# Six row tiles in the last FFN chunk, block 12 in Strassen form, and work moved across the chunk seams

## The chip, the cores and the metric

One core of one Trainium2 chip. The metric is the device time of one execution in microseconds, median over runs.

Names: PE is TensorE, DVE is VectorE, ACT is ScalarE, POOL is GpSimd. The FFN runs over 16 row tiles of 128 rows. I call its chunks 0 (tiles 0, 1), A (2 to 5), B (6 to 9), C (10 to 13) and D (14, 15); the change replaces C and D by one chunk E (10 to 15).

## The reference, cut to what matters

```python
x = A_x                                             # (1, 2048, 640), bf16
h = layernorm(x) * (1 + ca) + sa
x = x + ga * irfft2(rfft2(h) * (w_r + 1j * w_i))    # not touched (with LN2 and chunk 0 it fills the first 104 us)
h = layernorm(x) * (1 + cb) + sb                    # LN2
x = x + gb * ((silu(h @ w_gate) * (h @ w_up)) @ w_down)   # 640 -> 1728 -> 640
```

1728 hidden columns are 13 blocks of 128 (0 to 12) and 64 left over.

## The kernel before

Gate and up are computed together by a seven-product Strassen scheme: one 2x2 side is (gate, up), the other is the two halves of a chunk's rows; the sums of weights (`GS`, `UG`) are made once, the sums of row halves (`h_sums`) per chunk. Blocks 0 to 11 go through it in pairs; block 12 and the 64 columns (`gu13`) are done plainly. Down is Strassen again, over pairs of row tiles.

```python
chunks = [(0, 2), (2, 4), (6, 4), (10, 4), (14, 2)]     # first tile, number of tiles

def gate_up_pairs(ci, ATc, extra):
    n = chunks[ci][1]
    F, M = 8 // n, 64 * n          # blocks in a group, columns of a product
    nG = 12 // F
    # step(0) X = w*b11, copied out by ACT      step(1) Y = GS0*t1 + ..
    # step(2) X += GS1*t2, copied out           step(3) Z = w*b21 + ..,  DVE c11 = Z + c0
    # step(4) X += GS2*t3, copied out as c3,    DVE c22 = Y + c3
    # step(5) Y += GS3*b22 + ..,                DVE c12 = Y + c2
    # step(6) X += w*t4 + .., two silu (ACT),   DVE first half of rows = c11 * g21
    # step(7) DVE second half of rows = c12 * g22
    for p in range(nG):
        step(0, p); step(5, p - 2); step(4, p - 1); step(7, p - 2)
        if p and extra: extra.pop(0)()
        if p == 0: fin13 = gu13(ci, ATc)
        step(1, p); step(2, p); step(6, p - 1)
        if n == 4: queue(p - 1)              # sums for the down product, run in turns
        if p < nG - 1: step(3, p); run(8 // n)
        if p == 1: fin13()
    half = gu_plain(ci, ATc, 12, tmp[nG % 2])      # block 12, plain
    step(5, nG - 2); step(4, nG - 1); step(7, nG - 2); step(3, nG - 1)
    # ... (n == 2 has an order of its own)
    run(2); half(0); step(6, nG - 1); half(1, lambda: run(len(later)))
    # ...

for ci, (t0, n) in enumerate(chunks):
    # ... gate and up ...
    if ci == 1:                                    # LN2 variances of tiles 10 to 15
        ln2_var(10, 6); ln2_pow(10, 6); ln2_nb(10, 6)      # DVE, POOL, DVE
    if ci + 1 < len(chunks): ln2_tr(ci + 1)        # transposed load of the next chunk
    for j in range(n // 2):
        # a pair of tiles; in the last one DVE also runs ln2_mod and h_sums of the next chunk
        down_pair(ATc, t0 + 2 * j, j, nxt)
```

The PSUM banks are taken in turn from a ring of eight (`next_banks`).

## Time and profile before

252.05 us, median of three runs (251.85 to 252.06); the traced run took 250.93 us. The trace from A's first product on, one row a chunk; the columns are the stretch and its length, then busy time and (number) of PE, of PE's weight loads, of DVE, ACT and POOL, then the granted clock and the DMA's share and rate:

```profile
104.37:144.56 40.19, 40.19 (x331) 32.13 (x330) 35.82 (x76) 26.56 (x48) 8.12 (x7) 1.00 0.13 29
144.56:184.76 40.20, 40.20 (x331) 32.06 (x330) 35.27 (x77) 24.29 (x45) 5.42 (x6) 1.00 0.15 35
184.76:224.95 40.19, 40.19 (x332) 32.15 (x331) 33.29 (x75) 21.62 (x41) 5.43 (x6) 1.00 0.10 26
224.95:245.73 20.78, 20.68 (x284) 18.34 (x281) 16.50 (x41) 10.51 (x20) 0.00 (x0) 1.00 0.07 21
```

A, B and C take the same time although their DVE and ACT load differs by 2.5 and 5 us: PE sets it. D's two tiles cost 10.4 us each, the others' 10.05.

Before A's first product lie 104.37 us, after the last row 3.4 us for the last output and its transfer. The last row runs to the output add that follows D's last product; up to that product's end, at 245.70, D takes 20.75 us.

### The profile page before, as it was taken

How to read it: one execution, taken by the hardware profiler on the slowest of the kernel's cores; microseconds unless marked ns; L12 is line 12 of the kernel's file. 1: busy time of each engine (PE TensorE's matmuls, PEld its weight loads, DVE VectorE, ACT ScalarE, POOL GpSimd, SP SyncE). 2: the span in 40 equal slices, each digit the busy share in tenths (PEclk: the TensorE clock that was granted, in tenths of full speed). 3: DMA queues.
4: the chain of work that ended last, by engine and by line, in shares of the span. 5: the costliest groups of instructions: out<-in, count | busy, mean ns of one | idle time of the engine just before them, and what ended most of it. 6: DMA issues, size and time to landing. Idle time of an engine off the chain costs nothing.

```text
span 249.1 us, 6473 instructions
## 1 busy us (share of the span) xinstructions
PE 243.5 (98%) x2512; PEld 200.4 (80%) x2512; DVE 209.7 (84%) x524; ACT 162.7 (65%) x300; POOL 74.3 (30%) x122
## 2 busy tenths in 40 slices
PE   8999999999999999999999999999999999999994
PEld 3778877999889888688877778886768887779973
DVE  4798888998898997879997997879995888895895
ACT  3778666997788798488862487674356766235740
POOL 8487755894025422000003900001330000440000
PEclk9999999999999999999999999999999999999999
DMA  7999999999999999300005020003311000211001
GB/s 221 396 357 334 309 365 191 175 397 381 286 352 288 275 264 186 81 9 0 3 0 108 13 68 29 3 3 58 73 42 39 3 0 3 54 53 57 3 0 53
DMA packets 45760, 34.43 MB, mean 138 GB/s; under 512 B 21731, under 2 KB 42658, under 8 KB 45346
## 3 DMA queue, kind: packets, MB, share of 16 engines
q1 hardware_dynamic: 43936, 30.00, 42.8%
q0 software_dynamic: 1504, 3.95, 6.7%
q8 instruction: 19, 0.31, 0.5%
q10 hardware_dynamic: 290, 0.08, 0.1%
q14 instruction: 11, 0.09, 0.1%
HBM read 26.72 MB, written 4.72 MB: 126 GB/s over the span
## 4 chain that ended last, share of the span: by engine, by line
PE 80%; SPq 9%; DMA 6%; ACT 1%; DVE 1%; issue 1%; DVEq 0%; ACTq 0%
PE psum L1016 33%; PE psum L899 19%; PE psum L986 9%; DMA rW<-wflip_r 4%; PE psum L879 3%; PE psum L597 3%; PE psum L664 3%; PE psum L567 2%; SPq L273 2%; SPq L277 2%; PE psum L1149 2%; DMA rM<-in_w_mod_dram 2%; SPq L275 2%; PE psum L1152 2%; PE psum L974 2%; PE psum L618 2%
## 5 line engine op out<-in xcount | busy, mean ns | idle before, releaser
L1016 PEld LDWEIGHTS <-rW 128*128 128x128 bf16 (+1 forms) x528 | 46.9, 98 | 5.6 <-issue 0.2
L1016 PE MATMUL psum<-rW 128*128 128x256 bf16 (+1 forms) x240 | 27.1, 259 | 0.0
L913 POOL TENSOR_TENSOR rM<-rM,rL 128x320 f32<-128x320 f32 x6 | 5.9, 975 | 68.2 <-ACT rL L912 68.2
L899 PEld LDWEIGHTS <-rE 128*128 128x128 f16 (+1 forms) x196 | 19.1, 97 | 7.7
L1016 PE MATMUL psum<-rY,rW 128*128 128x256 bf16 (+1 forms) x96 | 24.0, 259 | 0.0
L986 PE MATMUL psum<-rW 128*128 128x256 bf16 (+1 forms) x170 | 23.1, 291 | 0.0
L899 PE MATMUL psum<-rE 128*128 128x320 f16 (+1 forms) x147 | 22.3, 299 | 0.0
L590 DVE TENSOR_TENSOR rM<-psum,rW 128x384 bf16<-128x384 f32 (+2 forms) x42 | 20.1, 541 | 2.0 <-PE psum L567 1.4
L986 PEld LDWEIGHTS <-rW 128*128 128x128 bf16 x170 | 16.6, 98 | 3.8
L1016 PEld LDWEIGHTS <-rE 128*128 128x128 f16 x192 | 17.4, 98 | 2.4
L899 PEld LDWEIGHTS <-rX 128*128 128x128 bf16 (+1 forms) x151 | 14.6, 97 | 5.4
L760 POOL TENSOR_TENSOR rstd<-rstd,mhalf 128x4 f32<-128x4 f32 (+2 forms) x4 | 4.5, 1120 | 48.2 <-DVE rstd L756 48.2
L1052 DVE TENSOR_TENSOR rH<-psum,rW 128x512 bf16<-128x512 f32 x21 | 14.5, 689 | 4.9 <-PE psum L1016 3.1
L1048 ACT COPY rH<-psum 128x512 f32<-128x512 f32 x21 | 12.3, 585 | 9.0 <-PE psum L1016 7.3
L1042 ACT COPY rW<-psum 128x512 f32<-128x512 f32 x21 | 12.3, 585 | 6.8 <-PE psum L1016 6.7
L1055 ACT COPY rX<-psum 128x512 f32<-128x512 f32 x21 | 12.3, 586 | 6.7 <-PE psum L1016 6.7
L1070 DVE TENSOR_TENSOR rX<-rH,rL 128x512 bf16<-128x512 bf16 x21 | 8.9, 423 | 9.1 <-ACT rL L1068 9.0
L382 DVE SCALAR_TENSOR_TENSOR rE<-rE,mv,psum 128x648 bf16<-128x648 f32 (+1 forms) x17 | 14.2, 844 | 2.1 <-PE psum L318 1.5
L1056 DVE TENSOR_TENSOR rX<-psum,rX 128x512 f32<-128x512 f32 x21 | 14.4, 685 | 1.7 <-ACT rX L1055 1.6
L899 PE MATMUL psum<-rA,rX 128*128 128x320 bf16 (+1 forms) x98 | 15.6, 299 | 0.0
L1016 PE MATMUL psum<-rH,rW 128*128 128x256 f16 (+1 forms) x96 | 15.1, 259 | 0.1
L1016 PE MATMUL psum<-rE,rY 128*128 128x256 f16 (+1 forms) x96 | 15.1, 259 | 0.0
(198 smaller groups left out, 674.3 us busy)
## 6 DMA issues: line engine op xcount, KB each, us to landing
out_dram<-rA SPq DMA_DIRECT2D x31, 80.0 KB, 1.6
rM<-in_w_mod_dram SPq DMA_DIRECT2D x3, 800.0 KB, 9.9
rX<-in_A_x_dram SPq DMA_DIRECT2D x3, 640.0 KB, 7.3
rA<-in_B_w_down_dram SPq DMA_DIRECT2D x2, 960.0 KB, 14.4
rM<-in_w_mod_dram SPq DMA_DIRECT2D x1, 1600.0 KB, 7.1
rY<-in_B_w_gate_dram POOLq DMA_DIRECT2D x2, 768.0 KB, 7.7
rW<-in_B_w_gate_dram SPq DMA_DIRECT2D x2, 640.0 KB, 7.2
rW<-in_B_w_up_dram SPq DMA_DIRECT2D x2, 640.0 KB, 6.5
```

What stands on the lines that cost most here:

```text
L382: nc.vector.scalar_tensor_tensor(Zv[:, h], Cv[:, h], mv[:, t, 0:1], zps[:, h], ALU.mult, ALU.subtract)
L590: nc.vector.tensor_tensor(PP[:, :, hl], xv[:, :, hl], in1, ALU.mult)
L597: nc.tensor.matmul(yps[:, i, :], lhsT=_rev(PP, 64 * n * ps + i, [[n, 128]]), rhs=identb[:], start=(ps == 1 and i == 0), stop=(ps == 0 and ...
L899: nc.tensor.matmul(o, lhsT=lhsT, rhs=rhs, start=start, stop=stop, skip_group_check=True)
L986: nc.tensor.matmul(gu[u], lhsT=Wgu[:, u, c5, ff * 128:(ff + 1) * 128], rhs=h2T[:, :, c5, :], start=(c5 == 0), stop=(c5 == NC5 - 1))
L1016: nc.tensor.matmul(o[:, f], lhsT=w, rhs=b, start=(start and f == 0 and i == 0), stop=(stop and f == F - 1 and i == len(ops) - 1), skip_gro ...
L1042: nc.scalar.copy(c0, X)
L1048: nc.scalar.copy(c2, X)
L1052: nc.vector.tensor_tensor(c11, Z, c0, ALU.add)
L1055: nc.scalar.copy(c3, X)
L1056: nc.vector.tensor_tensor(c22, Y, c3, ALU.add)
L1070: nc.vector.tensor_tensor(ato, v4(c11), v4(g21), ALU.mult)
```

## The change

The intent: give PE fewer and wider matmuls. C and D become one chunk of six tiles; block 12 joins the Strassen scheme as a group of its own at the head of each chunk; the first down products are begun between the last group's, where block 12's plain products had stood; the last variances move from A's down part into A's third group. Room for the larger chunk is found in the rows of x1 that are already output.

```diff
-    chunks = [(0, 2), (2, 4), (6, 4), (10, 4), (14, 2)]
+    chunks = [(0, 2), (2, 4), (6, 4), (10, 6)]
-    def gate_up_pairs(ci, ATc, extra):
+    def gate_up_pairs(ci, ATc, extra, dn):
-        F, M = 8 // n, 64 * n
-        nG = 12 // F
+        M = 64 * n
+        groups = [[12]] + ([[f, f + 6] for f in range(6)] if n == 4
+                           else [[f + 6 * s] for f in range(6) for s in range(2)])
+        L = len(groups) - 1
 ...
+            if p == 2 and ci == 1:
+                ln2_var(10, 6)
+                ln2_pow(10, 6)
 ...
-        half = gu_plain(ci, ATc, 12, tmp[nG % 2])
-        step(5, nG - 2)
-        step(4, nG - 1)
-        step(7, nG - 2)
-        step(3, nG - 1)
+        step(5, L - 1)
+        step(4, L)
+        step(7, L - 1)
+        step(3, L)
 ...
+            run(2)
+            dn = dn()
+            dn.head(0)          # down: X, blocks 0 to 3
+            step(6, L)
+            dn.head(1)          # X, blocks 4 and 6
+            run(len(later))
+            queue(L)
+            later.extend([lambda: step(8, L), lambda: step(7, L)])
+            step(5, L, True)
+            dn.head(2)          # Y, blocks 0 to 3
+            run(len(later))
 ...
+    def at_of(ci):
+        A = rM.cut(4096, [NFC * N]) if chunks[ci][1] == 6 else AT[:, 0:NFC * N]   # x1's rows
 ...
-        if ci == 1:
-            ln2_var(10, 6)
-            ln2_pow(10, 6)
-            ln2_nb(10, 6)
```

The rest is addresses, the 1664 columns of the tables in place of 1536, tiles 14 and 15 normalized and transposed during B, and a guard that drops four useless sums at the start of each chunk of four.

More of the change, by code (lines that the diff above doesn't have):

```diff
@@ L743, in adaln_block_kernel @@
     nb2 = const.tile([P, NT], F32, name="nb2")
-    h2T_first, h2T_next = rW.cut(45056, [2, NC5, 128]), rW.cut(33280 + 512, [4, NC5, 128])
-    xn2c = rL.cut(4096, [4, D])
-    chunks = [(0, 2), (2, 4), (6, 4), (10, 4), (14, 2)]
+    h2T_first, h2T_next = rW.cut(38912, [2, NC5, 128]), rW.cut(33280 + 512, [6, NC5, 128])
+    xn2c, xn2x = rL.cut(4096, [4, D]), rM.cut(5120, [2, D])
+    chunks = [(0, 2), (2, 4), (6, 4), (10, 6)]
     def ln2_sq(t):
@@ L770, in ln2_xn_act, with ln2_tr @@
         t = chunks[ci][0] + i
-        nc.scalar.activation(xn2c[:, i, :], x1[:, t, :], ACT.Identity, scale=rstd2[:, t:t + 1], bias=nb2[:, t:t + 1])
+        nc.scalar.activation(xn2c[:, i, :] if i < 4 else xn2x[:, i - 4, :], x1[:, t, :], ACT.Identity, scale=rstd2[:, t:t + 1], bias=nb2[:, t:t + 1])
     def h2T_of(ci):
         return (h2T_next if ci else h2T_first)[:, 0:chunks[ci][1]]
-    def ln2_tr(ci):
-        n = chunks[ci][1]
+    def ln2_tr(ci, lo=0):
+        n = min(chunks[ci][1] - lo, 4)
         nc.sync.dma_start_transpose(
-            h2T_of(ci).rearrange("p tl c q -> p (tl c) q"),
-            xn2c[:, 0:n].rearrange("p tl (c q) -> p (tl c) q", c=NC5))
+            h2T_of(ci)[:, lo:lo + n].rearrange("p tl c q -> p (tl c) q"),
+            (xn2x if lo else xn2c)[:, 0:n].rearrange("p tl (c q) -> p (tl c) q", c=NC5))
     def ln2_mod(ci, cs=range(NC5)):
@@ L793, in ln2_mod @@
                                      scale=one_p_cb[:, c5:c5 + 1], bias=modcols[:, 2, c5:c5 + 1])
-    GS = [r.cut(off, [2, 1536], F16) for r, off in ((rY, 0), (rE, 25600), (rW, 38912), (rE, 31744))]
-    UG = rH.cut(1280, [1536], F16)
+    GC = 13 * 128
+    GS = [r.cut(off, [2, GC], F16) for r, off in ((rY, 0), (rE, 25088), (rW, 42496), (rE, 31744))]
+    UG = rH.cut(1280, [GC], F16)
     def gu_w(u, k):
-        return Wgu[:, u, 2 * k:2 * k + 2, 0:1536]
+        return Wgu[:, u, 2 * k:2 * k + 2, 0:GC]
     def gu_table(i, q):
-        fs = slice(512 * q, 512 * q + 512)
+        fs = slice(512 * q, 512 * q + 512 if q < 2 else GC)
         s1, s2, s4 = (GS[k][:, :, fs] for k in (0, 1, 3))
@@ L810, in gu_dma @@
     def gu_dma(o, w, r, n, first):
-        nc.gpsimd.dma_start(o, w[128 * r:128 * r + 128 * n, 0:1536].rearrange("(c5 dp) f -> dp c5 f", dp=P),
+        nc.gpsimd.dma_start(o, w[128 * r:128 * r + 128 * n, 0:GC].rearrange("(c5 dp) f -> dp c5 f", dp=P),
                             accum_op=ALU.bypass if first else ALU.add)
@@ L826, in adaln_block_kernel @@
     S1, S2, S3, S4 = (rE.cut(17920 + 1792 * i, [HK, 128], F16) for i in range(4))
-    Hs = [rE.cut(37888 + 1024 * i, [2, 256], F16) for i in range(3)] + [rH.cut(0, [2, 256], F16)]
-    nh = rY.cut(6400, [4, 128])
-    tmp = [r.cut(off, [512], F32) for r, off in ((rW, 45056), (rW, 47104), (rH, 4352), (rH, 6400))]
+    H4 = [r.cut(off, [2, 256], F16) for r, off in ((rE, 38400), (rE, 39424), (rY, 6656), (rH, 0))]
+    H6 = [r.cut(off, [2, 384], F16) for r, off in ((rE, 38400), (rL, 4096), (rL, 5632), (rL, 7168))]
+    nh4, nh6 = rW.cut(41472, [4, 128]), rX.cut(14336, [6, 128])
+    tmp = [r.cut(off, [512], F32) for r, off in ((rM, 0), (rM, 2048), (rH, 4608), (rH, 6656))]
     c3f, c22f = rX.cut(16384, [512], F32), rX.cut(18432, [512], F32)
-    c11b, c12b = (rH.cut(8448 + 1024 * i, [512]) for i in range(2))
-    g21b, g22b = (rL.cut(1024 * i, [512]) for i in range(2))
+    c1b, g2b = rH.cut(8704, [2, 512]), rL.cut(0, [2, 512])
     B11, B21, B12, B22 = (Wd_sb[:, HK * i:HK * i + HK, 320 * j:320 * j + 320] for i, j in ((0, 0), (1, 0), (0, 1), (1, 1)))
@@ L891, in down_plain, with __init__, prod, head @@
             wd_tables(i, 0)
-    def down_pair(ATc, t, j, nxt):
-        X, Y, Z = (psum[:, next_banks(1), 0:320] for _ in range(3))
-        ta, tb = 256 * j, 256 * j + 128
-        xa, xb = x1[:, t, :], x1[:, t + 1, :]
-        def mm(o, lhsT, rhs, start=False, stop=False):
-            nc.tensor.matmul(o, lhsT=lhsT, rhs=rhs, start=start, stop=stop, skip_group_check=True)
-        def prod(o, lhs, rhs, start=False, stop=False, ks=range(HK)):
-            for k in ks:
-                mm(o, lhs[rows(k), k], rhs[rows(k), k], start and k == ks[0], stop and k == HK - 1)
-        A11, A12 = ATc[:, 0:HK, ta:ta + 128], ATc[:, HK:2 * HK, ta:ta + 128]
-        A22 = ATc[:, HK:2 * HK, tb:tb + 128]
+    class Down:
+        def __init__(self, ATc, t, j):
+            self.t, self.banks = t, [psum[:, next_banks(1), 0:320] for _ in range(3)]
+            ta, tb = 256 * j, 256 * j + 128
+            self.A11, self.A12 = ATc[:, 0:HK, ta:ta + 128], ATc[:, HK:2 * HK, ta:ta + 128]
+            self.A22 = ATc[:, HK:2 * HK, tb:tb + 128]
+        def prod(self, o, lhs, rhs, start=False, stop=False, ks=range(HK)):
+            for k in ks:
+                nc.tensor.matmul(o, lhsT=lhs[rows(k), k], rhs=rhs[rows(k), k], start=start and k == ks[0],
+                                 stop=stop and k == ks[-1], skip_group_check=True)
+        def head(self, i):
+            X, Y, Z = self.banks
+            if i == 0:
+                self.prod(X, self.A11, B11, True, ks=range(0, 4))
+            elif i == 1:
+                self.prod(X, self.A11, B11, ks=(4, 6))
+            else:
+                self.prod(Y, S1, T1, True, ks=range(0, 4))
@@ L907, in down_pair @@
+    def down_pair(dn, nxt, headed):
+        X, Y, Z = dn.banks
+        t, A11, A12, A22, prod = dn.t, dn.A11, dn.A12, dn.A22, dn.prod
+        xa, xb = x1[:, t, :], x1[:, t + 1, :]
         last = t + 2 == NT
         add = (nc.vector if last else nc.gpsimd).tensor_tensor
-        prod(X, A11, B11, True, ks=range(0, 6))
-        prod(Z, A12, B21, True, ks=range(0, 2))
-        prod(X, A11, B11, stop=True, ks=range(6, HK))
+        if headed:
+            prod(X, A11, B11, stop=True, ks=(5,))
+            prod(Z, A12, B21, True, ks=range(0, 2))
+        else:
+            prod(X, A11, B11, True, ks=range(0, 6))
+            prod(Z, A12, B21, True, ks=range(0, 2))
+            prod(X, A11, B11, stop=True, ks=range(6, HK))
@@ L916, in down_pair @@
             prod(W, A22, T4, True, ks=range(0, 3))
-        prod(Y, S1, T1, True, True)
+        prod(Y, S1, T1, not headed, True, ks=range(4 if headed else 0, HK))
         nxt(0)
@@ L957, in h_sums @@
         b11, b12, b21, b22 = h_parts(ci)
-        t1, t2, t3, t4 = (h[:, :, 0:64 * n].rearrange("p c (t q) -> p c t q", q=128) for h in Hs)
+        t1, t2, t3, t4 = (h.rearrange("p c (t q) -> p c t q", q=128) for h in (H6 if n == 6 else H4))
         tt = nc.vector.tensor_tensor
@@ L966, in h_neg, with gu13 @@
     def h_neg(ci):
-        nc.scalar.mul(nh[:, 0:chunks[ci][1]], h2T_of(ci)[:, :, 4], -1.0)
-    def gu13(ci, ATc):
-        n = chunks[ci][1]
+        nc.scalar.mul((nh6 if chunks[ci][1] == 6 else nh4)[:], h2T_of(ci)[:, :, 4], -1.0)
+    def gu13(ci, ATc, lo=0, hi=2):
         h2T = h2T_of(ci)
-        g13 = psum[:, next_banks(1), 0:128 * n]
+        q = slice(128 * lo, 128 * hi)
+        g13 = psum[:, next_banks(1), 0:128 * (hi - lo)]
         for c5 in range(NC5):
-            nc.tensor.matmul(g13, lhsT=Wp13[:, c5, :], rhs=h2T[:, :, c5, :], start=(c5 == 0), stop=(c5 == NC5 - 1))
-        sg13 = rX.cut(14336, [512], F32, parts=64)[:, 0:128 * n]
+            nc.tensor.matmul(g13, lhsT=Wp13[:, c5, :], rhs=h2T[:, lo:hi, c5, :], start=(c5 == 0), stop=(c5 == NC5 - 1))
+        sg13 = rX.cut(512 * lo if chunks[ci][1] == 6 else 14336, [128 * (hi - lo)], F32, parts=64)
         nc.scalar.activation(sg13, g13[0:64], ACT.Silu)
-        return lambda: nc.vector.tensor_tensor(ATc[0:64, 13, :], g13[64:128], sg13, ALU.mult)
+        return lambda: nc.vector.tensor_tensor(ATc[0:64, 13, q], g13[64:128], sg13, ALU.mult)
     def gu_plain(ci, ATc, ff, sg):
@@ L982, in gu_plain, with half @@
         gu = [psum[:, next_banks(1), 0:N] for _ in range(2)]
-        def half(u, between=lambda: None):
+        def half(u):
             for c5 in range(NC5):
@@ L990, in half @@
             else:
-                between()
                 k = 6 if ff == 12 else ff + ff // 6
@@ L996, in gu_plain @@
         return half
-    def gate_up_pairs(ci, ATc, extra):
+    def gate_up_pairs(ci, ATc, extra, dn):
         n = chunks[ci][1]
-        F, M = 8 // n, 64 * n
-        nG = 12 // F
+        M = 64 * n
+        groups = [[12]] + ([[f, f + 6] for f in range(6)] if n == 4 else [[f + 6 * s] for f in range(6) for s in range(2)])
+        L = len(groups) - 1
         b11, b12, b21, b22 = h_parts(ci)
         h2T = h2T_of(ci)
+        nh = nh6 if n == 6 else nh4
+        c1x = rX.cut(4096, [2, M]) if n == 6 else rM.cut(4096, [2, M])
         ha, hb = h2T[:, 0:n // 2, 4], h2T[:, n // 2:n, 4]
         nha, nhb = nh[:, 0:n // 2], nh[:, n // 2:n]
-        t1, t2, t3, t4 = (h[:, :, 0:M] for h in Hs)
-        A4 = ATc.rearrange("p (s f) q -> p s f q", s=2)
+        t1, t2, t3, t4 = H6 if n == 6 else H4
         st = {}
         def mms(o, g, parts, start, stop):
-            for f in range(F):
-                ff = F // 2 * g + f % (F // 2) + 6 * (f // (F // 2))
+            for f, ff in enumerate(groups[g]):
                 fs = slice(128 * ff, 128 * ff + 128)
@@ L1015, in mms, with v, bank, at @@
                 for i, (w, b) in enumerate(ops):
-                    nc.tensor.matmul(o[:, f], lhsT=w, rhs=b, start=(start and f == 0 and i == 0), stop=(stop and f == F - 1 and i == len(ops) - 1),
-                                     skip_group_check=True)
-        def v(ap):
-            return ap.rearrange("p (f q) -> p f q", f=F)
-        def flat(ap):
-            return ap.rearrange("p f q -> p (f q)")
-        def bank():
-            return v(psum[:, next_banks(1), :])
+                    nc.tensor.matmul(o[:, f], lhsT=w, rhs=b, start=(start and f == 0 and i == 0),
+                                     stop=(stop and f == len(groups[g]) - 1 and i == len(ops) - 1), skip_group_check=True)
         def step(i, g, sep=False):
-            if not 0 <= g < nG:
+            if not 0 <= g <= L:
                 return
+            F = len(groups[g])
+            def v(ap):
+                return ap[:, 0:F * M].rearrange("p (f q) -> p f q", f=F)
+            def bank():
+                return v(psum[:, next_banks(1), :])
+            def at(h):
+                f, s = groups[g][0] % 6, groups[g][0] // 6
+                return ATc.rearrange("p (s f) q -> p s f q", s=2)[:, s:s + F, f, M * h:M * h + M]
             c0, c2 = v(tmp[g % 2]), v(tmp[2 + g % 2])
-            c3, c22, c11, c12, g21, g22 = (v(x) for x in (c3f, c22f, c11b, c12b, g21b, g22b))
+            cb = c1b if g else c1x
+            c3, c22, c11, c12, g21, g22 = (v(x) for x in (c3f, c22f, cb[:, 0], cb[:, 1], g2b[:, 0], g2b[:, 1]))
             X, Y, Z = st.setdefault(g, [None] * 3)
-            ato, atb = (A4[:, :, F // 2 * g:F // 2 * g + F // 2, M * h:M * h + M] for h in range(2))
-            def v4(ap):
-                return ap.rearrange("p (s f) q -> p s f q", s=2)
             if i == 0:
@@ L1058, in step @@
                 mms(Y, g, [(GS[3], b22), (UG, hb)], False, True)
-                if sep:
-                    return
-                nc.vector.tensor_tensor(c12, Y, c2, ALU.add)
+                if not sep:
+                    nc.vector.tensor_tensor(c12, Y, c2, ALU.add)
             elif i == 8:
@@ L1064, in step @@
             elif i == 7:
-                nc.vector.tensor_tensor(atb, v4(c12), v4(g22), ALU.mult)
+                if g:
+                    nc.vector.tensor_tensor(at(1), c12, g22, ALU.mult)
+                else:
+                    for o, r in ((ATc[0:RK, 6], slice(0, RK)), (ATc[64:RK, 13], slice(RK, P))):
+                        nc.vector.tensor_tensor(o.rearrange("p (h q) -> p h q", h=2), cb[r, :, 0:M], g2b[r, :, 0:M], ALU.mult)
             else:
@@ L1069, in step @@
                 nc.scalar.activation(g22, c22, ACT.Silu, scale=-1.0)
-                nc.vector.tensor_tensor(ato, v4(c11), v4(g21), ALU.mult)
+                if g:
+                    nc.vector.tensor_tensor(at(0), c11, g21, ALU.mult)
         later = []
         def queue(g):
-            if g % 2:
-                ks = slice(g - 1, g + 1 + g // (nG - 1))
+            f = groups[g][-1] - 6
+            if 0 < f < 6 and f % 2:
+                ks = slice(f - 1, f + 1 + f // 5)
                 later.extend(lambda q=q: a_sum(ATc, 0, q, ks) for q in range(4))
@@ L1082, in run @@
                 k -= 1
+        if n == 6:
+            nc.gpsimd.memset(ATc[RK:P].rearrange("p (s f) q -> p s f q", s=2)[:, :, 6, :], 0.0)
         fin13 = None
-        for p in range(nG):
+        for p in range(L + 1):
             step(0, p)
@@ L1091, in gate_up_pairs @@
                 extra.pop(0)()
+            if p == 2 and ci == 1:
+                ln2_var(10, 6)
+                ln2_pow(10, 6)
             if p == 0:
-                fin13 = gu13(ci, ATc)
+                fin13 = gu13(ci, ATc, 0, 3 if n == 6 else n)
+            if p == 2 and n == 6:
+                fin13 = gu13(ci, ATc, 3, 6)
             step(1, p)
             step(2, p)
-            if n == 2 and p == 2:
-                for q in (0, 2, 1, 3):
-                    a_sum(ATc, 0, q, slice(0, 2))
             step(6, p - 1)
-            if n == 4:
+            if p:
                 queue(p - 1)
-            if p < nG - 1:
+            if p < L:
                 step(3, p)
                 run(8 // n)
-            if p == 1:
+            if p == 1 or p == 3 and n == 6:
                 fin13()
-        half = gu_plain(ci, ATc, 12, tmp[nG % 2])
-        step(5, nG - 2)
-        step(4, nG - 1)
-        step(7, nG - 2)
-        step(3, nG - 1)
-        if n == 2:
-            step(6, nG - 1)
-            step(5, nG - 1, True)
-            half(0)
-            r1, r2, r3, r4 = (lambda q=q: a_sum(ATc, 0, q, slice(2, 6)) for q in range(4))
-            q1, q2, q3, q4 = (lambda q=q: a_sum(ATc, 0, q, slice(6, 7)) for q in range(4))
-            step(8, nG - 1)
-            half(1)
-            step(7, nG - 1)
-            later[:] = [r1, half.rest, q1, r2, q2, r4, q4, r3, q3]
-        else:
-            run(2)
-            half(0)
-            step(6, nG - 1)
-            half(1, lambda: run(len(later)))
-            later.append(half.rest)
-            queue(nG - 1)
-            later.extend([lambda: step(8, nG - 1), lambda: step(7, nG - 1)])
-            step(5, nG - 1, True)
-        run(len(later))
+        step(5, L - 1)
[7 more added lines that the diff above has]
+        dn.head(1)
+        run(len(later))
+        queue(L)
[3 more added lines that the diff above has]
+        run(len(later))
+        return dn
     def at_of(ci):
         N = 128 * chunks[ci][1]
-        return AT[:, 0:NFC * N].rearrange("p (f q) -> p f q", f=NFC)
+        A = rM.cut(4096, [NFC * N]) if chunks[ci][1] == 6 else AT[:, 0:NFC * N]
+        return A.rearrange("p (f q) -> p f q", f=NFC)
     if True:
@@ L1186, in adaln_block_kernel @@
         if ci:
-            gate_up_pairs(ci, ATc, [lambda i=i: (ln2_xn_act(2, i), wd_tables(i, 1)) for i in range(4)] + [lambda: wd_tables(3, 0)] if ci == 1 else [])
+            extra = {1: [lambda i=i: (ln2_xn_act(2, i), wd_tables(i, 1)) for i in range(4)] + [lambda: wd_tables(3, 0), lambda: ln2_nb(10, 6)],
+                     2: [lambda: None, lambda: ln2_xn_act(3, 4), lambda: (ln2_xn_act(3, 5), ln2_tr(3, 4))]}.get(ci, [])
+            dn = gate_up_pairs(ci, ATc, extra, lambda: Down(ATc, t0, 0))
         else:
@@ L1222, in nxt @@
             def nxt(i):
-                if j == 0:
-                    if n == 4 and i < 4:
-                        a_sum(ATc, 1, i)
-                elif i == 0:
-                    ln2_mod(ci + 1)
-                    h_sums(ci + 1)
-                if j and i != 1 and ci + 2 < len(chunks):
-                    q = (0, 3, 2, 4).index(i)
-                    if q < chunks[ci + 2][1]:
-                        ln2_xn_act(ci + 2, q)
-                if j and i == 4:
-                    h_neg(ci + 1)
-            down_pair(ATc, t0 + 2 * j, j, nxt)
+                if 2 * j + 2 < n:
+                    if i < 4:
+                        a_sum(ATc, j + 1, i)
+                elif ci + 1 < len(chunks):
+                    if i == 0:
+                        ln2_mod(ci + 1)
+                        h_sums(ci + 1)
+                    if i != 1 and ci + 2 < len(chunks):
+                        ln2_xn_act(ci + 2, (0, 3, 2, 4).index(i))
+                    if i == 4:
+                        h_neg(ci + 1)
+            down_pair(Down(ATc, t0 + 2 * j, j) if j else dn, nxt, j == 0)
 @with_exitstack
```

## The prediction

> **What bounds the kernel now.** I read the page first (busy shares and the slices), then the chain of work that ended last, in order of time, then the timelines of VectorE (DVE) and ScalarE (ACT) at the seams between chunks. I call the FFN chunks by letters: A is row tiles 2 to 5, B 6 to 9, C 10 to 13, D 14 and 15. The change replaces C and D by one chunk E of six tiles.
>
> The page:
>
> ```profile
> PE 243.5 (98%) x2512; PEld 200.4 (80%) x2512; DVE 209.7 (84%) x524; ACT 162.7 (65%) x300; POOL 74.3 (30%) x122
> PE   8999999999999999999999999999999999999994
> PEclk9999999999999999999999999999999999999999
> ```
>
> TensorE (PE) is busy in every slice at an undisturbed clock. A busy PE could still hide waits, so the chain has to say whether they cost anything. Its lines are start, length, engine and source line; L1016 are the Strassen products of gate and up, L974 the last 64 columns, L986 block 12 done plainly, L899 the down products:
>
> ```profile
> 104.37 0.44 PE psum L1016 x4
> 104.81 1.08 PE psum L974 x5
> 105.89 21.83 PE psum L1016 x200
> 127.72 1.08 PE psum L986 x5
> ...
> 131.19 13.37 PE psum L899 x98
> 144.56 0.44 PE psum L1016 x4
> ...
> 184.76 0.44 PE psum L1016 x4
> ...
> 211.58 13.37 PE psum L899 x98
> 224.95 0.45 PE psum L1016 x8
> 225.40 0.55 PE psum L974 x5
> 225.94 8.50 PE psum L1016 x152
> ...
> 235.02 0.63 ACT rL L1069
> 235.65 0.58 ACT rX L1055
> 236.23 0.04 issue
> 236.27 1.58 PE psum L1016 x24
> 237.86 1.09 PE psum L986 x10
> 238.95 6.75 PE psum L899 x53
> ...
> 245.73 0.33 DVE rA L871
> ```
>
> A runs from 104.37 to 144.56, 40.19 us, B and C take the same, and each is a chain of matmuls back to back. D (224.95 to 245.73) is the only one in which ACT enters. So from A on, the time is the number of matmuls times their spacing. The chain gives the spacing by width: 128 columns 8.50/152 = 55.9 ns, 256 columns 21.83/200 = 109.2 ns, 320 columns 13.37/98 = 136.4 ns, 512 columns 1.08/5 = 216 ns.
>
> **What the Trainium skill says.** "TensorE: Matmul & The Clock Gate", section Back-to-back issue gap, gives N/2.4 + 2.5 ns for a warm matmul, but says that in a stream with weight loads 128 columns take some 81 ns and 512 some 131 ns. This trace agrees with the formula (55.8 and 215.8 ns) and not with the stream figures. There is no row of 384 columns here, so I take 384/2.4 + 2.5 = 162.5 ns, an estimate from that page that the four measured widths support. "PSUM — Partial Sum Buffer", section The four PSUM rules, limits a matmul output to one bank, 512 fp32; a product over three tiles is 384 wide, so E gets one feed-forward block a group where A has two. "VectorE: DVE Perf Modes", section The TRN2 errata, says that each instruction pays a fixed part, here visible as 0.69 us at 512 columns from PSUM and 0.48 at 320 (0.21 us for 192 columns, so some 0.14 fixed). Nearly half as many columns again per instruction therefore suits DVE better than D's, but E has 12 groups of 384 and one of block 12, where C and D had nine of 512.
>
> **The change part by part.**
> A group of one block is seven products: 2+3+2+3+2+3+3 = 18 matmuls.
>
> 1. Block 12 in Strassen, A and B. Removed: 10 matmuls of 512, 10 x 0.216 = 2.16 us. Added: 18 of 256, 18 x 0.1092 = 1.97. Per chunk -0.19, for both -0.39 us, all on PE's path.
> 2. C and D become E. Removed, gate and up: C 211.58 - 184.76 = 26.82, D 238.95 - 224.95 = 14.00, together 40.82. Added: 13 blocks x 18 = 234 matmuls of 384, and twice 5 for the last 64 columns, 244 x 0.1625 = 39.65. That is -1.17. It splits thus: 94,464 columns become 93,696 (0.32 us at 2.4 columns a ns), 462 matmuls become 244 (218 x 2.5 ns = 0.55), and D's own waits go (14.00 less 216 x 0.0559 and 15 x 0.109, that is 0.29).
> 3. Down: three pairs before, three after, the last one in the same order; 13.37 + 6.75 us stay. The head (X blocks 0 to 3, then 4 and 6, then Y blocks 0 to 3) moves ten matmuls between the last group's products. It adds none. It has to cover what block 12 covered: ten wide matmuls, 2.16 us, stood around the last group while ACT and DVE finished it.
> 4. The variances: the three small DVE operations, the power on POOL and the row of shifts go from A's down into A's third group. In A's down DVE idled 1.44 us for POOL there. PE did not wait for it, so this is worth nothing on the path by itself.
> 5. DVE also loses four sums of 128 columns at the start of each chunk of four tiles (the old queue took group -1 for odd) and two operations of block 12 at the end (0.69 us each), and gains three adds of 256 and two products for block 12 at the start. The sixth and fifth tile's normalization and their transpose go into B, where DVE and ACT have room (22.5 and 18.8 us busy of 26.8).
> 6. The tables are 1664 wide for 1536: DVE adds 256 more columns in two operations in chunk 0, some 0.13 us each at the 2x rate seen there (1024 columns 0.68 us). DVE idles 0.35 us before its last block, so it fits. DMA is nearly idle by then.
>
> Sum on PE: -0.39 - 1.17 = -1.56 us.
>
> **What is given back.** Three places where slack gets thin.
>
> ```profile
> 166.90 0.42 DVE L1070 TENSOR_TENSOR rX<-rH,rL 128x512 bf16<-128x512 bf16 x1 [0.66 <-ACT rL L1068]
> 170.77 0.69 DVE L993 TENSOR_TENSOR rX<-psum,rW 96x512 bf16<-96x512 f32 x1
> 171.49 0.69 DVE L995 TENSOR_TENSOR rX<-psum,rW 32x512 bf16<-32x512 f32 x1
> ```
>
> The end of A and B. From the start of the last turn, PE's spacings put the end of its last gate product at 6.22 us, then head, product, head, and X block 5 at 7.70 and Y block 4 at 8.11. ACT starts 0.26 us after a product's end (124.06 to 124.32 in the timeline) and its silu of 0.60 is done at 7.08. DVE comes to the first of these products free, as the 0.66 us of idle shows, then works through add (0.60 from start to start), add, product (0.34), add, two sums (0.20 each) and reaches the last product at 7.15; done 7.57, first sum done near 8.0. PE wants them at 7.70 and 8.11. It fits by about 0.1 us: I count 0.1 of stall each.
>
> Inside E. X is one bank that must be copied out before its next product. After the third product of X, ACT's copy is ready 0.26 + 0.475 (between 0.42 at 320 and 0.585 at 512) + 0.05 = 0.79 us later; PE has five matmuls to do, 0.81. It fits by 0.03. I count 0.1 over all groups.
>
> The start of E. Six tiles make the shift-and-scale (0.65 us each of five in B's down, under POOL's adds) and the five sums of halves half again as long, some 1.9 us more. DVE starts them some 1.3 us sooner, because block 12's two operations no longer stand at the head of its queue. PE wanted them 1.3 us after they were ready. I count 0.1.
>
> Together 0.4 us: 252.05 - 1.56 + 0.4 = 250.9.
>
> **The rivals.**
> 1. The seam stalls: with the plain block gone the head is too short, and PE waits for silu, product and sum at each of three chunk ends. For: the working leaves 0.1 us. Against: DVE idles just before. It would give back 0.3 to 0.6 us a seam: 251.3 to 252.2.
> 2. ACT becomes the bound in E: five instructions of 384 for 18 matmuls, some 2.4 us of 2.93, 82% (five of 0.59, 2.96 of 3.93, 75% in A). The X copy then costs each group 0.1: 1.3 us back, 252.1. For: the 0.03 us. Against: ACT issues overlap, 0.49 apart for 0.60.
> 3. Everything fits and D's waits were worth more: 250.5.
> 4. The DVE queue of E's start is late by a whole microsecond: 251.9. Against: its idle time elsewhere.
>
> None of them reaches 2%, which would be 247.0 or 257.1; PE's work is only 1.56 us less.
>
> **Range and chances.** 250.9 us, 250.2 to 252.0 eight times in ten: the low end is all of the gain and 0.3 us between runs, the high end rivals 1 or 2 nearly whole. Faster by over 2%: 0.01, as no such time stands on the chain. Within 2%: 0.97. Slower by over 2%: 0.02, for an order of waits that I overlooked in the reused rows.
>
> **What would show it.** In the changed chain, A and B should be 40.0 us each; E some 59.8 from start to the last down product; matmuls of 384 columns spaced 162 to 163 ns. The seams show as ACT or DVE pieces before the first L899 group; rival 2 as small repeated pieces of ACT inside E; rival 4 as a piece of DVE before E's first products. If the 384-wide spacing is well above 163 ns, or E takes over 61 us, I am wrong.

## The result, and the profile after

249.96 us median of six runs (249.41 to 250.82), the kernel before in the same rounds 251.66 (250.64 to 252.06); ratio 0.9942, 95% interval 0.9913 to 0.997. Within 2%. The median itself lies 0.24 us below the low end of the predicted range (250.2), but the kernel before also ran faster in these rounds than the 252.05 us from which the range was worked out; 0.9942 of 252.05 is 250.6, inside it. A second set of six runs gave 250.36 us and 0.9938 (0.9915 to 0.996).

The chain of the changed kernel from A on (start, length, what; L1032 are the gate and up products, L990 the 64 columns, L903 down):

```profile
104.42 0.22 PE psum L1032 x2
...
105.72 24.02 PE psum L1032 x220
...
131.86 12.55 PE psum L903 x92
144.41 0.22 PE psum L1032 x2
...
184.45 0.33 PE psum L1032 x2
...
185.59 5.01 PE psum L1032 x30
...
191.41 31.93 PE psum L1032 x196
...
225.13 19.35 PE psum L903 x145
...
244.51 0.32 DVE rA L872
```

No ACT or DVE piece is left between A's first product and the last output: the chain is PE alone. The chunks, in the columns of before, and then the page's line of busy times:

```profile
104.42:144.41 39.99, 39.99 (x339) 32.83 (x338) 37.25 (x79) 27.71 (x52) 6.78 (x7) 1.00 0.15 30
144.41:184.45 40.04, 40.04 (x339) 32.77 (x337) 33.36 (x70) 25.41 (x49) 5.46 (x6) 1.00 0.19 43
184.45:244.49 60.04, 60.02 (x396) 38.19 (x393) 48.79 (x109) 34.73 (x78) 7.61 (x7) 1.00 0.06 19
```

```profile
PE 242.3 (98%) x2310; PEld 189.7 (77%) x2310; DVE 208.6 (84%) x516; ACT 167.7 (68%) x325; POOL 75.7 (31%) x123
```

A lost 0.20 us, B 0.16, and E takes 60.04 where C and D took 60.94 up to their last product (184.76 to 245.70). Together 141.33 - 140.07 = 1.26 us, 0.5% of 251.66. The runs show 0.6%, and their interval holds both. (The expectations below have 141.36, 60.97 and 0.93, because I had taken D to the add.) PE is busy 98% before and after, with 2310 instructions for 2512: its busy share says nothing of the gain, the number and width of its matmuls do. A's first product stood at 104.37 before; in traces of kernels that are alike up to there it fell anywhere from 104.1 to 106.1 us in fast runs, and at 107.4 in one single look. The two traced runs of the changed kernel took 249.69 and 251.38 us, and their first products of A stood at 104.42 and 106.12: the whole difference. The noise between runs therefore lies largely ahead of the change, while the chunks repeat to a few hundredths, and I read the experiments by chunk.

### The profile page after: what moved, and what is told of

Read it like the earlier page. It is cut to its first block, busy times and chain, and to the rows that moved or that the text cites. A ratio compares the mean times of both kernels' runs of the same rounds, so it can differ in the third digit from the quotient of the medians.

```text
span 247.9 us, 6123 instructions
## 1 busy us (share of the span) xinstructions
PE 242.3 (98%) x2310; PEld 189.7 (77%) x2310; DVE 208.6 (84%) x516; ACT 167.7 (68%) x325; POOL 75.7 (31%) x123
## 4 chain that ended last, share of the span: by engine, by line
PE 81%; SPq 10%; DMA 6%; DVE 1%; ACT 1%; issue 1%; DVEq 0%; ACTq 0%
PE psum L1032 36%; PE psum L903 19%; PE psum L1002 6%; DMA rW<-wflip_r 4%; PE psum L880 3%; PE psum L597 3%; PE psum L664 3%; PE psum L567 2%; SPq L273 2%; SPq L275 2%; SPq L277 2%; PE psum L1165 2%; DMA rM<-in_w_mod_dram 2%; PE psum L1168 2%; SPq L279 2%; PE psum L990 2%
## 5 line engine op out<-in xcount | busy, mean ns | idle before, releaser
L1032 PEld LDWEIGHTS <-rW 128*128 128x128 bf16 (+1 forms) x429 | 42.0, 98 | 12.6
L1032 PE MATMUL psum<-rW 128*128 128x256 bf16 (+1 forms) x247 | 42.2, 287 | 0.0
L903 PEld LDWEIGHTS <-rE 128*128 128x128 f16 (+1 forms) x196 | 19.0, 97 | 7.8
L903 PE MATMUL psum<-rE 128*128 128x320 f16 (+1 forms) x147 | 22.9, 299 | 0.0
L1070 ACT COPY rX<-psum 128x384 f32<-128x384 f32 (+2 forms) x27 | 14.0, 519 | 7.5 <-PE psum L1032 7.4
L1032 PEld LDWEIGHTS <-rE 128*128 128x128 f16 x156 | 15.3, 98 | 4.7
L1063 ACT COPY rH<-psum 128x384 f32<-128x384 f32 (+2 forms) x27 | 14.0, 517 | 7.0 <-PE psum L1032 6.3
L1067 DVE TENSOR_TENSOR rH<-psum,rM 128x512 bf16<-128x512 f32 (+1 forms) x24 | 15.0, 624 | 4.1 <-PE psum L1032 2.2
L1086 ACT ACTIVATE rL<-psum 128x384 bf16<-128x384 f32 (+2 forms) x27 | 14.4, 532 | 5.5 <-PE psum L1032 3.4
L1071 DVE TENSOR_TENSOR rX<-psum,rX 128x384 f32<-128x384 f32 (+2 forms) x27 | 16.3, 604 | 1.6 <-ACT rX L1070 1.4
L1057 ACT COPY rM<-psum 128x384 f32<-128x384 f32 (+2 forms) x27 | 13.9, 515 | 4.0 <-PE psum L1032 3.9
L1032 PE MATMUL psum<-rW,rE 128*128 128x256 bf16 (+1 forms) x78 | 15.6, 290 | 0.0
L1032 PE MATMUL psum<-rE,rY 128*128 128x256 f16 (+1 forms) x78 | 15.6, 290 | 0.0
L1087 ACT ACTIVATE rL<-rX 128x384 bf16<-128x384 f32 (+2 forms) x27 | 15.1, 558 | 0.0
L1170 DVE SCALAR_TENSOR_TENSOR rM<-psum,rX 128x640 f32<-128x640 f32 x16 | 13.1, 821 | 1.8 <-PE psum L1168 1.7
L1002 PE MATMUL psum<-rW 128*128 128x256 bf16 x130 | 14.4, 273 | 0.0
L872 DVE TENSOR_TENSOR rA<-psum,rM 128x320 bf16<-128x320 f32 (+1 forms) x27 | 12.1, 470 | 2.4 <-PE psum L880 2.3
```

The costliest lines, as they stand in the source:

```text
L903: nc.tensor.matmul(o, lhsT=lhs[rows(k), k], rhs=rhs[rows(k), k], start=start and k == ks[0], stop=stop and k == ks[-1], skip_group_check=True)
L1002: nc.tensor.matmul(gu[u], lhsT=Wgu[:, u, c5, ff * 128:(ff + 1) * 128], rhs=h2T[:, :, c5, :], start=(c5 == 0), stop=(c5 == NC5 - 1))
L1032: nc.tensor.matmul(o[:, f], lhsT=w, rhs=b, start=(start and f == 0 and i == 0), stop=(stop and f == len(groups[g]) - 1 and i == len(ops) - ...
L1057: nc.scalar.copy(c0, X)
L1063: nc.scalar.copy(c2, X)
L1067: nc.vector.tensor_tensor(c11, Z, c0, ALU.add)
```

## The experiments

Each chunk is counted from its first product to the next chunk's first, E to the last down product, in the times of the chain; where the chain does not pass through a first product, its start in the timeline is used, which lies 0.16 us earlier throughout and is corrected for that. No run was 2% faster or slower than the kernel before. All but one kernel agreed with the reference; in two the agreement hid a mistake.

| run | A | B | rest | time, ratio to before |
|---|---|---|---|---|
| before | 40.19 | 40.20 | C 40.19, D 20.75 | |
| changed | 39.99 | 40.04 | E 60.04 | 249.96, 0.9942 |
| block 12 plain, mended | 40.57 | 40.19 | E 60.28 | 251.24, 0.9983 (0.9966 to 0.9999) |
| C and D, mended | 40.00 | 40.04 | C 40.19, D 20.76 | 251.75, 0.9996 (0.9966 to 1.0027) |
| no head | 40.65 | 40.65 | E 60.25 | 251.43, 0.997 (0.9917 to 1.0023) |
| wide copy | 40.00 | 40.04 | E 60.83 | 253.43, one look |
| variances late | 40.00 | 41.59 | E 60.03 | 252.25, one look |
| plain and late | 40.69 | 40.50 | E 60.28 | 251.48, one look |
| order in E, banks swapped (wrong result) | 40.00 | 40.04 | E 59.94 | 250.24, 0.9945 (0.993 to 0.996) |
| changed, again | 40.00 | 40.04 | E 60.03 | 250.36, 0.9938 (0.9915 to 0.996) |
| banks swapped, again | 40.00 | 40.04 | E 59.89 | 249.91, 0.9922 (0.9902 to 0.9942) |

### The two halves of the gain, and a mistake in both

First I took back one half at a time: A and B with the old function (block 12 plain, no head), E new; then A and B new, C and D with the old function.

```diff
-            dn = gate_up_pairs(ci, ATc, extra, lambda: Down(ATc, t0, 0))
+            if n == 4:
+                gate_up_old(ci, ATc, extra)      # the function of before
+                dn = Down(ATc, t0, 0)            # and down_pair(.., headed=False)
+            else:
+                dn = gate_up_pairs(ci, ATc, extra, lambda: Down(ATc, t0, 0))
```

> Chunks A and B (tiles 2 to 5, 6 to 9) exactly as in the kernel before, block 12 plain and down not begun early; the six-tile chunk E as in the changed kernel. Theory (the gain is PE's own work, additive by chunk): in the chain A and B go from 39.99 and 40.04 us back to 40.19 each, together +0.35; E stays at 60.0; against the kernel before the time is about 1.0 us less, ratio 0.996. Rival (most of the gain comes from the heads and the Strassen block 12, the merge gives little): A and B unchanged from before but E loses its gain too, ratio 0.999 or more.

> A and B as in the changed kernel, but the last six tiles as chunks C (four) and D (two) with the code of before. Theory: C 40.19 and D 20.8 us, together 60.97, against 60.04 for E; so 0.93 us longer than the changed kernel and only 0.35 shorter than before, ratio to before 0.9985. Rival (the merge gives little): C and D together end up within 0.2 us of E.

Both passed the comparison, with 250.27 us (0.9939, interval 0.9859 to 1.002) and 251.07 us (0.9958, 0.9906 to 1.0011). But A came out at 39.76 us, less than either kernel, which no theory allows. The chain showed why: L990 took 0.55 us for its five matmuls where 512 columns take 1.08. The old function called `gu13` with the new default of two tiles, so the 64 left-over columns of half the rows were stale, an error small enough for the tolerance. Half-done work found only by counting microseconds: the two runs' times are void. Mended:

```diff
-                fin13 = gu13(ci, ATc)
+                fin13 = gu13(ci, ATc, 0, n)
```

> The first run of A and B with block 12 plain left the last 64 columns of two of each chunk's four tiles uncomputed by my mistake (five matmuls of 256 columns in place of 512, 0.54 us too little per chunk). Mended here. Theory: A and B 40.2 to 40.3 each (39.76 and 39.67 plus 0.54), together 0.35 to 0.5 more than the changed kernel; E at 60.0 to 60.3. Rival (the merge's gain needs the Strassen block 12 of A and B): E 60.5 or more.

> The same mistake stood in the first split run, in C only. Mended. Theory: C 40.19 (39.65 + 0.54) and D 20.8, together 60.95 against 60.04 for E, and A and B at 40.0 each. Rival: C and D within 0.2 us of E.

The split came out as expected to 0.04 us:

```profile
184.15 0.44 PE psum L1167 x4
...
224.34 0.45 PE psum L1167 x8
```

C is 224.34 - 184.15 = 40.19, D 20.76, 60.95 together against 60.03 and 60.04 for E in two traces. The merge is worth 0.91 us by itself, and keeping A and B new does not change it.

Block 12 plain gave B 40.19, the whole of its gain back, but A 40.57: 0.38 more than in the kernel before. The chain of that A is a long row of DVE pieces. The edit had kept the variances in A's third group, on top of all that DVE did there before, so I guessed that they were what was too much; that is tested below. E was 60.28, with one wait of 0.25 us in its middle at an ACT copy that began late; it came back in all three kernels with the old A and B, at the same copy, and the trace names nothing that the copy waited for. That stays open.

### The head

```diff
-        dn.head(0)
         step(6, L)
-        dn.head(1)
 ...
         step(5, L, True)
-        dn.head(2)
```

> The changed kernel with the ten early down products of each chunk put back behind the last group. Theory (they cover the silu, product and sum of the last group): in A and B block 5 of X then starts 0.68 us after the last gate product's follower and PE waits some 0.6 us there for DVE, so A and B are 40.6 each, with a DVE piece in the chain just after the first five down products; E does not need the head, since its last group is block 11 and X reads only blocks 0 to 6, so E stays within 0.1 of 60.04. In all +1.2 us, ratio to before 0.999. Rival (the order does not matter, DVE is ahead anyway): A and B stay at 40.0.

A and B took 40.65 us each, 0.66 and 0.61 more, as expected. The chain at A's end:

```profile
129.37 0.59 ACT rX L1070
...
129.99 0.69 DVE rX L1071
...
132.01 0.35 DVE rX L1089
...
132.40 12.87 PE psum L903 x93
```

ACT's copy, then DVE's add (L1071), left out here its product, next add and two sums, then the last group's product (L1089), and then PE: the same row that the prediction worked through, with PE now at its end. Of E I had expected nothing; it took 0.21 us more, and its end lost more than that, since its first 30 products took 4.88 us for 5.01 (that wait is the subject of a section below). At E's end the last product of X came 0.30 us late, before ACT's copy of X was out: the copy began 0.26 us after the product before it had ended and took 0.48, and only 0.49 us of products were left in between, since the head had stood there too. DVE's next add then held PE for another 0.11 us. So the head covers two waits, that for silu, product and sum in the chunks of four and that for the copy in E.

### The copy out of X, 0.03 us of slack

In E a PE product follows ACT's copy at once. From the changed kernel, a steady group (ACT, then PE's product that needs X):

```profile
220.75 0.48 ACT L1070 COPY rX<-psum 128x384 f32<-128x384 f32 x1 [0.35 <-PE psum L1032]
```

```profile
221.31 0.49 PE L1032 MATMUL psum<-rL,rW 128*128 128x384 f16 x2
```

The copy ends at 221.23; with the 0.05 us from a copy's end to the product that waited for it (224.76 to 224.81 in the run without the head), 0.03 are left. I made the copy read the whole bank:

```diff
-                nc.scalar.copy(c3, X)
+                if n == 6:
+                    nc.scalar.copy(c3f, st[g][3])     # X's bank, 512 columns for 384
+                else:
+                    nc.scalar.copy(c3, X)
```

> The changed kernel with one copy of ACT in each group of E (the one out of X before its last product) made to read the whole bank of 512 columns, 128 of them unused; it takes 0.585 for 0.48 us and nothing else changes. Theory (the copy is ready 0.03 us before PE needs it, so 0.11 more is felt): PE waits some 0.07 us in each of 11 groups, E 60.04 + 0.8 = 60.8. Rival (the slack is larger than I worked out, or the spacing already hides a wait): E stays within 0.15 of 60.04.

E took 60.83, 0.79 more (a single look at a granted clock of 0.992, but its A and B took the usual 40.00 and 40.04); the 196 products that took 31.93 us in the chain took 32.72:

```profile
194.37 32.72 PE psum L1032 x196
```

One instruction 0.11 us longer (0.586 for 0.48), off the chain in every view of the changed kernel, and the kernel pays 0.08 us ten times: in ten groups the product that needs X starts 0.242 us after the one before it, where 0.162 is usual. The slack was as thin as worked out. Does it cost anything as it is? The other way round, with room (this kernel also has the swapped banks of the next section, with which E takes 59.89):

```diff
+            if n == 6 and p < L:
+                step(3, p)          # ahead of step(6), which needs the copy
             step(6, p - 1)
```

> The changed kernel with the swapped banks and, in E, the fourth step's product put ahead of the seventh's, so that ACT's copy has 1.30 us of matmuls to hide behind in place of 0.81. Theory (the copy just fits, so room adds nothing): E 59.9, the spacing of 384 columns stays at 162.9 ns, the time as with the swapped banks alone within the noise. Rival (waits too short for the chain are inside the 162.9 ns): the spacing falls to 162.5 or less and E by over 0.1 us more.

E 59.94 for 59.89, its 196 products 31.96 us for 31.92: no gain. This kernel's result is wrong (relative error 0.025): DVE then writes the next c11 before the old one is read, from the one buffer it has. The kinds, sizes and order of matmuls are those of a right one, so the time stands as evidence, not as a version to keep. The copy just fits.

Nor does the 31.93 us hold many small waits. Of the changed kernel's 196 products nearly all start 0.162 or 0.163 us after the one before; one comes 0.24 us after, in the last group's turn:

```profile
221.64 0.33 PE L1032 MATMUL psum<-rX,rW 128*128 128x384 bf16 x1
221.88 0.48 PE L1032 MATMUL psum<-rW,rE 128*128 128x384 bf16 x2
```

DVE's add that reads that product's bank (L1071) ends at 221.82, and five products that stand between in the earlier turns are missing here. The wait is 0.08 us, too short to show as a piece of the chain, and the second trace repeats it. It shows only when the starts are read one by one.

### The wait at E's start

The changed kernel's longest wait in E: PE's second group (0.14 us between the end of the product issued at 187.05, two of 0.163 us, and the next at 187.52), and DVE at the same time:

```profile
187.05 0.49 PE L1032 MATMUL psum<-rL,rW 128*128 128x384 f16 x2
187.52 0.48 PE L1032 MATMUL psum<-rE,rY 128*128 128x384 f16 x2
```

```profile
179.99 3.36 DVE L789 TENSOR_SCALAR rW<-rW,one_p_cb,modcols 128x768 bf16<-128x768 bf16 x5
...
186.59 0.88 DVE L872 TENSOR_TENSOR rA<-psum,rM 128x320 bf16<-128x320 f32 x2
```

PE starts 0.05 us after DVE's last output add of B (186.59 + 0.88 = 187.47). Going round the ring of eight, that Y gets the bank of B's last X. Swapping two banks:

```diff
-            self.t, self.banks = t, [psum[:, next_banks(1), 0:320] for _ in range(3)]
+            self.t, bk = t, [psum[:, next_banks(1), 0:320] for _ in range(3)]
+            self.banks = [bk[1], bk[0], bk[2]]
```

> The changed kernel with X and Y of a down pair swapped in their PSUM banks. In the changed kernel PE waits 0.15 us in E's second group, at 187.4 us, where DVE finishes the last output adds of B. Theory: that product of Y takes over the bank of B's last X, the last of the four outputs to be added; with the banks swapped it gets the bank of Y, read first, and the wait goes: E 59.9, 0.15 less, the time itself unchanged within the noise. Rival (it waits for the half sums or ACT's copy): the 0.15 us stay.

E 59.89 and the first 30 products 4.88 us for 5.01: the wait is gone, so it was the bank and not the sums of halves. That run's time was 250.11 us (0.9924, 0.987 to 0.9978). With five rounds each, side by side:

> The changed kernel once more, for the size of the gain with more rounds and beside the next run. Theory: from A's first product to the last down product 140.07 us as in its first trace (141.36 before), ratio to before 0.994 to 0.996; the rest of what runs differ by lies ahead of A. Rival: A, B or E differ from the first trace by over 0.1 us.

> The changed kernel with the banks of X and Y of a down pair swapped, once more and with more rounds: E 59.9, 0.15 us less than the changed kernel, so a time 0.1 to 0.2 us less at best, which the rounds may not resolve.

The changed kernel repeated its chunks to 0.01 us. The swapped one took E down to 59.89 again and ran in 249.91 us against 250.36; the trace accounts for 0.14 of that, the intervals of the ratios (0.9902 to 0.9942 and 0.9915 to 0.996) overlap, and the rest is noise as far as these runs tell. By the trace it beats both kernels.

### The variances

> The changed kernel with the last six LN2 variances, their power and their row of shifts put back behind A's last group. Theory (they were never on PE's path, and with block 12 in Strassen A's DVE has room for them): A and B stay at 40.0, E at 60.0, each within 0.1 us; DVE idles some 1.4 us for POOL in A's down again. Rival (moving them is what keeps B's start free): B's first products wait, B 40.2 or more.

```diff
-            if p == 2 and ci == 1:
-                ln2_var(10, 6)
-                ln2_pow(10, 6)
 ...
+        if ci == 1:                 # behind A's last group, as before
+            ln2_var(10, 6)
+            ln2_pow(10, 6)
+            ln2_nb(10, 6)
```

My theory fell: B took 41.59 us, 1.55 more. PE's two longest waits in B's first groups:

```profile
147.60 0.39 PE L1032 MATMUL psum<-rE 128*128 128x256 f16 x2 [0.58 <-DVE rE L979]
...
149.53 0.38 PE L1032 MATMUL psum<-rE,rY 128*128 128x256 f16 x2 [0.55 <-DVE rA L872]
```

L979 is the last operation on the half sum t2, L872 the output adds that free a bank, as at E's start. DVE waited 1.44 us for POOL's power during A's down, POOL's adds then came later and collided with DVE's sums, and everything that DVE prepares for B slid. In the kernel before, with the same order, PE had not waited. DVE's line and PE's need there:

```profile
146.22 0.29 DVE L963 TENSOR_SCALAR rE<-rE 128x512 f16<-128x512 f16 x1
```

```profile
146.57 0.61 PE L1016 MATMUL psum<-rE 128*128 128x256 f16 x4
```

Ready at 146.51, used at 146.57, right after the product before it: no wait, but since 0.05 to 0.06 us pass from a DVE operation's end to the product that waited for it (149.47 to 149.53 above), no slack either. The changed kernel's first group is block 12 alone, so PE wants t2 after 0.22 + 1.08 + 0.33 = 1.63 us of B for 0.44 + 1.08 + 0.65 = 2.17 before. DVE was no later than before: t2 was ready 42.15 us after A's first product here, 42.14 there. PE came for it 0.54 us earlier because the group is shorter and 0.19 earlier because A is, and waited 0.74. The early variances are what pays for that: in the changed kernel t2 is ready at 144.59, 1.28 us ahead of its use at 145.87.

The last run asks whether the variances were also what slowed A when block 12 was plain:

> A and B with block 12 plain, as in the mended run, but with the variances behind A's last group as in the kernel before. That run's A took 40.57 us, 0.38 more than before, with a long row of DVE pieces in the chain. Theory (the variances, some 0.5 us of DVE put into A's third group, on top of the old block 12 and the old queue of sums, are what DVE could not take): A returns to 40.2, B 40.2, E 60.0 to 60.3. Rival (something else of the new layout slows A): A stays at 40.5.

The edit is the one above on top of the mended plain run. Half right: A's gate and up took 26.82 us (27.20 with the variances in it, 26.82 before), so they were. But A's down and B's start now lost 0.5 and 0.3 us to DVE, A 40.69 and B 40.50, although A and B do what they did before, in its order. DVE's sums under POOL's adds took 1.36, 1.10, 1.14 and 1.28 us here for 0.61, 1.10, 1.10 and 1.28 in the trace of before. The first pair met in the other order: before, DVE's sum came first and POOL's add took 1.31 us; here POOL's add kept its 0.85 and the sum took 1.36. With no slack, how two engines' instructions happen to meet decides; why they met so in this one look is not shown. Whether the kernel before itself loses such a wait in some of its runs I cannot say: there is one trace of it.

## Why the prediction was right, and where its steps were not

- The size. Predicted -1.56 us on PE with 0.4 given back, net -1.15, 250.9 us. The traces give -1.26; the medians, 249.96 against 251.66 and 250.36 against 251.91, give 0.3 to 0.4 more, which the chunks do not show and which lies within the intervals.
- Block 12 in A and B: predicted -0.39, measured -0.36 (39.99 and 40.04). With block 12 plain B returned to 40.19.
- C and D into E: predicted -1.17, measured -0.90 by the chain and -0.91 by the split. The terms of the sum were right: products of 384 columns are 162.5 ns apart where nothing waits, the figure taken, and D's own waits were 0.22 and 0.09 us, 0.31 for the 0.29 subtracted. The 0.27 between are three new waits of E, 0.14 at the bank, 0.08 in the last group's turn and 0.05 at ACT's copy of the first down product. So of the 0.4 us that were to be given back, PE gave back 0.3, nearly all in E, and for other reasons than those named.
- Down otherwise unchanged: 0.54 + 0.27 + 19.35 = 20.16 us for E, 20.12 predicted; the rest is the wait at that copy.
- The seams fit by about 0.1: no wait at A's end, 0.05 at B's (12.60 us for 92 down products, 12.55 in A), again at the copy of a down product. Taking the head away showed the row of work that it covers.
- Inside E, slack of 0.03: exact, by the wide copy.
- "It is worth nothing on the path by itself", of the variances, is the step that failed. It was read off the kernel before, where PE indeed did not wait; but t2 was ready just as PE could take it, the same change shortens the first group, and without the early variances B costs 1.55 us more. The total was right only because the change holds both.
- "DVE starts them some 1.3 us sooner" failed too, and was saved by a second error. The five scalings began at 179.99 us, before at 180.04: the operations of block 12 were gone, but the last product of the group, which used to come before them, now came later (171.72 for 170.32), and POOL's adds set the pace of the rest. And they took 3.36 us for 768 columns, hardly more than 3.25 for 512, where I had added half: POOL's three adds ran beside them both times. "SBUF — State Buffer" of the Trainium skill, section Who interferes with whom, says that DVE in a mode that uses two ports shares one pair with GpSimd, that the one that issues first has it for the whole instruction, and that such scalings can run in that mode. The trace agrees with the exclusion: alone five of 512 columns take 1.69 us (0.32 each from start to start, in the late-variances run, after POOL's last add), under POOL's adds 3.25. The data came in time, but with less to spare: t2 was ready at 185.40 for its use at 185.91, 0.51 us ahead, where C's had been 1.90 ahead (184.87 for 186.77, not the 1.3 that I had read).
- "Nearly half as many columns again per instruction" was a misreading: E's operations on DVE and ACT have 384 columns where C's and D's had 512. Nothing hung on it: DVE is busy 48.79 us in E for 49.79 in C and D, ACT 34.73 for 32.13.
- The rivals: stalls at the seams and ACT as the bound did not come; a late DVE at E's start did, as 0.14 us and through a PSUM bank, not through the data that I had named.

## What to carry to other kernels

When one engine is busy back to back, count its instructions and their measured spacing by width; that sum was good to 0.3 us of 141 here. Then look for slack, not for waits: an engine that nobody waits for may have no slack left, and a move that is worth nothing in the old order can be what makes the new one possible. And a chunk that comes out faster than the sum allows is a reason to look for work left undone, even when the result passes.

## What the Trainium skill lacked or had wrong

- "TensorE: Matmul & The Clock Gate", section Back-to-back issue gap: it says that in a stream of weight loads and matmuls 128 columns take some 81 ns and 512 some 131, and calls N/2.4 + 2.5 ns the isolated gap. In these streams, each matmul with its own weight load, the formula holds: 55.9 ns at 128 columns, 109.2 at 256, 162.5 at 384 (waits left out), 216 at 512; 81 and 131 appear nowhere.
- No page I found gives the two hand-overs that decide such a pipeline: from the issue slot's end of a product's last matmul (256 or 384 columns) to the start of the ACT copy that reads it 0.20 us for two of the copies (L1057, L1063) and 0.25 to 0.26 for the third (L1070), and from the end of an ACT or DVE instruction to the PE product that waited for it 0.05 to 0.06 us.
- "SBUF — State Buffer", section Who interferes with whom, states the shared port and who waits, but gives no duration for such a pair: sums of 896 columns with both inputs in SBUF took 0.61 to 0.63 us alone or ahead of POOL's add, and 1.10 to 1.36 when POOL was adding 128x320 fp32.
